# Accumulating w2 as two lines in four column tiles, storing them over two queues, and awaiting the output behind the closing barrier

## The chip, the cores and the metric

The kernel runs on one core of a Trainium2 chip. The metric is the device time of one execution in microseconds (us); a kernel's time is the median of its runs. The times in the profile count from the first instruction of the profiled execution; its span is about 1.3 to 2 us shorter than the measured time.

The names of the parts, as the kernel and the profile have them: PE is the matrix engine, DVE the vector engine, ACT the scalar engine, GpSimd (POOL) a further engine that has little to do here (6.0 us busy in the kernel before). SP issues transfers (DMAs) and waits for them; the profile counts them on 16 DMA engines. PE's sums stand in the tiles named ps, which the kernel puts into PSUM; it puts the other operands into SBUF. A drain is an engine's wait for its own work to end (DVE's of the kernel before starts at 419.7 us and lasts 0.32 us, over its last operation, 419.73 to 420.01); the closing barrier is the point at the end of the kernel's block that each engine passes only when all have come to it. The granted clock is the share of PE's full clock that it was given (0.50 or 1.00 in each record).

## The reference

One decode step of a transformer block, batch 2, one query position: a modulated layer norm, grouped attention over a cache of 32768 keys and values, and a two-layer MLP. Cut to what matters here:

```python
mod = (_silu(c) @ w_mod).reshape(c.shape[0], 6, 1, -1)      # sa, ca, ga, sb, cb, gb
...
x = x + ga * _A_ref(h, A_k_cache, A_v_cache, A_wq, A_wo)
h = _layernorm(x, axis=-1) * (1 + cb) + sb
x = x + gb * _B_ref(h, B_w1, B_b1, B_w2, B_b2)              # w1: 1024 x 3584, w2: 3584 x 1024
return x                                                    # (2, 1, 1024) bf16, 4 KB
```

## The kernel before

All weights and the cache come in pieces of up to 2 MB through one DMA queue, issued by SP, into a ring of 160 KB per partition. A loop over the eight (batch, group) pairs does the attention; behind it stand, fully unrolled, wo, two layer norms, w1, the gelu and w2. The change touches the last of these. The pieces of w2 (the last full one holds slices 16 to 23, the two small ones 24 to 26 and 27):

```python
    w2_v = B_w2.rearrange("(q p j) n -> p q (j n)", p=128, j=4)
    for k, off in enumerate((80, 112, 128)):
        add(("w2", k), [2, 4 * DM], w2_v[:, 2 * k:2 * k + 2, :], off * KB)
    add(("w2", 3), [3 * DM], w2_v[:, 6, 0:3 * DM], 144 * KB)
    add(("w2", 4), [DM], w2_v[:, 6, 3 * DM:4 * DM], 150 * KB)
```

w2 itself: the first 16 slices of 128 rows are multiplied with N = 512 into four column tiles of one PSUM bank, copied to SBUF and turned into columns; the last 12 slices are multiplied as columns, with the weights as the stationary operand, 96 matmuls of 2 columns:

```python
    for q in range(4):
        it = need("w2", q // 2)
        for j in range(4):
            for hf in range(2):
                t = 2 * (j % 2) + hf
                pe(lambda e, w=it.view, q=q, j=j, hf=hf, t=t: e.matmul(psS[0][32 * t:32 * t + 32, :], lhsT=gT[:, 4 * q + j, :],
                                                                       rhs=w[:, q % 2, j * DM + hf * 512:j * DM + (hf + 1) * 512],
                                                                       start=(q == 0 and j < 2), stop=(q == 3 and j >= 2), skip_group_check=True),
                   reads=[it.reg, "gT"], writes=["psS0"], mark=(j == 3 and hf == 1))
    load_row("dve", psS[0], "psS0", 3)
    to_columns(psO, "psO", 3, True, False)
    for q in range(4, 7):
        for j in range(4):
            it = need("w2", 2 if q < 6 else 3 if j < 3 else 4)
            w = it.view.rearrange("p a n -> p (a n)") if q < 6 else it.view
            for k in range(KT8):
                lo = ((q - 4) * 4 + j if q < 6 else j if j < 3 else 0) * DM + k * 128
                pe(lambda e, w=w, q=q, j=j, k=k, lo=lo: e.matmul(psO[:, 2 * k:2 * k + 2], lhsT=w[:, lo:lo + 128], rhs=gT[:, 4 * q + j, 0:2],
                                                                 start=False, stop=(q == 6 and j == 3), skip_group_check=True),
                   reads=[it.reg, "gT"], writes=["psO"], mark=(q > 4 and j in (2, 3) and k == KT8 - 1))
```

Then the gate, the residual, a turn into 16 rows, and the store, which SP awaits inside the block, ahead of the block's closing barrier:

```python
    dve(lambda e: e.tensor_tensor(mT[:, :, :], psO[:, 0:16].rearrange("p (k b) -> p k b", b=2), mod(5), ALU.mult), reads=["psO", "modT"], writes=["mT"])
    dve(lambda e: e.tensor_tensor(res_bf.rearrange("p b k -> p k b"), mT[:, :, :], x1b[:, :, :], ALU.add), reads=["mT", "x1b"], writes=["res_bf"])
    pe(lambda e: e.matmul(psM[0:16, 0:128], lhsT=res_bf.rearrange("p b k -> p (b k)"), rhs=ident[:, :], start=True, stop=True),
       reads=["res_bf", "ident"], writes=["psM"])
    dve(lambda e: e.tensor_copy(res16[:, :], psM[0:16, 0:128]), reads=["psM"], writes=["res16", "c16"])

    s_out = nc.alloc_semaphore("s_out")
    T.wait("sp", reads=["res16"])
    T.raw("sp", lambda e: e.dma_start(out.rearrange("b o (k p) -> (b o k) p", p=128), res16[:, :]).then_inc(s_out, 16))
    T.raw("sp", lambda e: e.wait_ge(s_out, 16))

    with nc.Block() as block:
        T.emit(block)
```

`x1b` (the residual plus the gated bias) is computed ahead of this on DVE; the biases are turned by PE at k == 1 of the w1 stage.

## Time and profile before

| | before |
|---|---|
| median | 423.7 us (423.6 to 423.91) |
| span of the profiled execution | 421.8 us |
| share of the queue that loads, of 16 engines' span | 99.1% |
| last full w2 piece landed | 415.98 us |
| last w2 matmul ended | 418.90 us |
| store issued, landed, span ended | 420.04, 421.44, 421.83 us |

From the page of the kernel before: two of the queues (packets, MB, share of 16 engines' span), and the shares of the chain of work that ended last.

```profile
q1 hardware_dynamic: 14322, 178.29, 99.1%
q8 instruction: 9, 0.15, 0.1%
...
DMA 80%; PE 16%; ACT 2%; SPq 1%; issue 0%; DVE 0%
```

The stream of loads (q1) is the bound.

The chain that ended last, in order of time (start us, us, what), its end:

```profile
385.85 30.13 DMA w<-in_B_w_dram
...
416.02 2.88 PE psO L757 x96
...
419.73 0.28 DVE c L764
```

DMA up to 415.98 us, then 96 matmuls, then (left out up to the last) three DVE operations and one matmul in a row, then the store. The issues of the last loads and of the store (KB each, us from issue to landing):

```profile
w<-in_B_w_dram SPq DMA_DIRECT2D x3, 2048.0 KB, 30.6
w<-in_B_w_dram SPq DMA_DIRECT2D x1, 768.0 KB, 28.0
w<-in_B_w_dram SPq DMA_DIRECT2D x1, 256.0 KB, 23.8
...
out_dram<-c SPq DMA_DIRECT2D x1, 4.0 KB, 1.4
```

And what the instruction queue moved from 416 to 418.6 us (packets, MB, share of 16 engines over the stretch):

```profile
q8 instruction: 1, 0.02, 2.4%
```

One packet falls in this stretch, behind the landing at 415.98; from 412 to 416 us there is none, and the load queue has 98.8% to itself. The packet's share, 2.4% of 16 engines over 2.6 us, is 1.0 us of one engine's time (0.024 x 16 x 2.6).

### The profile page before, as it was taken

Reading aid. Unit: us, or ns where it says so; the run is one execution under the profiler, and the core shown is the slowest. Engines: PE = TensorE matmul, PEld = TensorE weight load, DVE = VectorE, ACT = ScalarE, POOL = GpSimd, SP = SyncE. Lnnn points to the kernel's source line nnn. Section 1 sums busy time; section 2 is a strip of 40 time slices with the busy share of each in tenths; the row PEclk is TensorE's granted clock in tenths of the full one; section 3 lists DMA queues with packets and bytes.
Section 4 is the critical chain, followed back from the end, with each engine's and each line's share of the span. In section 5 each row is a group of like instructions: output and inputs, shape, how many; then the busy total and the mean of one; then the engine's idle time right before and its main releaser. Section 6 shows DMA issues by size and latency. Waiting matters only on the chain.

```text
span 421.8 us, 11638 instructions
## 1 busy us (share of the span) xinstructions
PE 299.5 (71%) x5171; PEld 238.1 (56%) x5171; DVE 167.1 (40%) x347; ACT 156.6 (37%) x269; POOL 6.0 (1%) x31
## 2 busy tenths in 40 slices
PE   1547478878997688587877848796888682445576
PEld 1105158866975678476767828684776671112244
DVE  1102026644663476155534724652474352101311
ACT  2000025547645349142833633383447245000020
POOL 3000000000000000000000000000000000000000
PEclk9999999969989999796988997898899696655565
DMA  8999999999999999999999999999999999999995
GB/s 334 429 431 423 435 432 423 429 432 426 433 432 429 435 429 430 435 429 429 435 429 432 437 423 433 435 426 433 433 428 433 430 430 435 427 429 424 428 423 244
DMA packets 14335, 178.47 MB, mean 423 GB/s; under 512 B 1513, under 2 KB 1520, under 8 KB 2802
## 3 DMA queue, kind: packets, MB, share of 16 engines
q1 hardware_dynamic: 14322, 178.29, 99.1%
q8 instruction: 9, 0.15, 0.1%
q14 instruction: 4, 0.03, 0.0%
HBM read 178.28 MB, written 0.00 MB: 423 GB/s over the span
## 4 chain that ended last, share of the span: by engine, by line
DMA 80%; PE 16%; ACT 2%; SPq 1%; issue 0%; DVE 0%
DMA K<-in_A_k_cache_dram 60%; PE psKT L542 11%; DMA wo<-in_A_wo_dram 8%; DMA w<-in_B_w_dram 7%; DMA wmod<-in_w_mod_dram 4%; PE psS L554 3%; ACT E_sb L575 1%; PE psO L584 1%; SPq L415 1%; ACT KT_sb L546 1%; PE psO L757 1%; PE psS L678 0%; ACT L575 0%; PE psM L565 0%; ACT S_sb L558 0%
## 5 line engine op out<-in xcount | busy, mean ns | idle before, releaser
L542 PE MATMUL psKT<-ident,K 128*128 128x128 bf16 x2048 | 173.8, 237 | 39.0 <-DMA K<-in_A_k_cache_dram 37.8
L542 PEld LDWEIGHTS psKT<-ident,K 128*128 128x128 bf16 x2048 | 133.2, 106 | 49.7 <-DMA K<-in_A_k_cache_dram 44.9
L548 DVE COPY KT_sb<-psKT 128x1024 bf16<-128x1024 bf16 x160 | 108.3, 689 | 112.5 <-PE psKT L542 112.5
L546 ACT ACTIVATE KT_sb<-psKT 128x1024 bf16<-128x1024 bf16 x96 | 98.0, 1020 | 131.2 <-PE psKT L542 131.2
L554 PE MATMUL psS<-qcur,KT_sb 128*128 128x8 bf16 x2048 | 88.2, 167 | 8.1 <-ACT KT_sb L546 6.7
L554 PEld LDWEIGHTS psS<-qcur,KT_sb 128*128 128x128 bf16 x2048 | 79.5, 99 | 13.2 <-ACT KT_sb L546 8.1
L584 PE MATMUL psO<-V,E_sb 128*32 128x512 bf16 x512 | 35.5, 403 | 6.3 <-DMA V<-in_A_v_cache_dram 5.0
L575 ACT ACTIVATE E_sb<-S_sb,negm 128x256 bf16<-128x256 f32 x64 | 32.3, 504 | 7.7 <-DVE negm L571 6.8
L559 DVE TENSOR_REDUCE m1c<-psS 128x8 f32<-128x512 f32 x32 | 22.1, 691 | 14.4 <-ACT S_sb L558 13.3
L558 ACT ACTIVATE S_sb<-psS 128x512 f32<-128x512 f32 x32 | 19.0, 592 | 14.1 <-PE psS L554 14.1
L584 PEld LDWEIGHTS psO<-V,E_sb 128*32 128x32 bf16 x512 | 11.5, 100 | 16.8 <-DMA V<-in_A_v_cache_dram 5.7
L491 PE MATMUL psS<-wmod,inT 128*32 128x512 bf16 x64 | 8.4, 622 | 11.9 <-DMA wmod<-in_w_mod_dram 11.9
L678 PE MATMUL psS<-wo,atT 128*32 128x512 bf16 x64 | 7.6, 627 | 11.3 <-DMA wo<-in_A_wo_dram 11.3
L462 ACT ACTIVATE stat<-stat 128x2 f32<-128x2 f32 x3 | 0.6, 204 | 38.9 <-DVE stat L461 38.9
L512 PE MATMUL psS<-wq,inT 128*32 128x512 bf16 x64 | 7.6, 627 | 6.9 <-DMA wq<-in_A_wq_dram 5.9
L575 ACT ACTIVATION_READ_ACCUMULATOR E_sb<-S_sb,negm 128x1 f32 x64 | 12.1, 189 | 0.0
L491 PEld LDWEIGHTS psS<-wmod,inT 128*32 128x32 bf16 x64 | 1.3, 112 | 17.9 <-DMA wmod<-in_w_mod_dram 17.4
L678 PEld LDWEIGHTS psS<-wo,atT 128*32 128x32 bf16 x64 | 1.9, 128 | 16.3 <-DMA wo<-in_A_wo_dram 10.3
L604 PE MATMUL psM<-msum,hmat 128*128 128x128 f32 x16 | 4.4, 359 | 7.1 <-DVE msum L599 7.1
L497 ACT ACTIVATE S_sb<-psS 128x512 f32<-128x512 f32 x1 | 0.6, 597 | 22.8 <-DVE S_sb L499 22.8
L499 DVE COPY S_sb<-psS 128x512 f32<-128x512 f32 x1 | 0.7, 692 | 20.6 <-PE psS L491 20.6
L599 DVE SCALAR_TENSOR_TENSOR msum<-psO,mk,msum 128x128 f32<-128x128 f32 x24 | 8.4, 351 | 0.8
(116 smaller groups left out, 132.3 us busy)
## 6 DMA issues: line engine op xcount, KB each, us to landing
K<-in_A_k_cache_dram SPq DMA_DIRECT2D x32, 2048.0 KB, 31.6
V<-in_A_v_cache_dram SPq DMA_DIRECT2D x32, 2048.0 KB, 35.1
wmod<-in_w_mod_dram SPq DMA_DIRECT2D x8, 1536.0 KB, 16.5
wq<-in_A_wq_dram SPq DMA_DIRECT2D x4, 2048.0 KB, 37.5
wo<-in_A_wo_dram SPq DMA_DIRECT2D x4, 2048.0 KB, 29.0
w<-in_B_w_dram SPq DMA_DIRECT2D x4, 1792.0 KB, 39.1
w<-in_B_w_dram SPq DMA_DIRECT2D x3, 2048.0 KB, 30.6
w<-in_B_w_dram SPq DMA_DIRECT2D x1, 768.0 KB, 28.0
```

What stands on the lines that cost most here:

```text
L491: pe(lambda e, w=it.view, k=k, ch=ch, n=n, q=q: e.matmul(bank[n][32 * q:32 * q + 32, :], lhsT=inT[:, k, :], rhs=w[:, ch * 512:(ch + 1) * 512],
L512: pe(lambda e, w=it.view, k=k, ch=ch, n=n, q=q: e.matmul(bank[n][32 * q:32 * q + 32, :], lhsT=inT[:, k, :], rhs=w[:, k % 2, ch * 512:(ch + ...
L542: pe(lambda e, kq=kq, jj=jj, w=it.view, t=t: e.transpose(psKT[kq][:, jj * 128:(jj + 1) * 128], w[:, t, :], ident[:, :]), reads=[it.reg, "i ...
L546: act(lambda e, src=src: e.activation(KT_sb[g8][:, :, :], src, ACT.Copy), reads=[f"psKT{kq}"], writes=[f"KT_sb{g8}"], sem=f"ev{cc}_{g8}")
L548: dve(lambda e, src=src: e.tensor_copy(KT_sb[g8][:, :, :], src), reads=[f"psKT{kq}"], writes=[f"KT_sb{g8}"], sem=f"ev{cc}_{g8}")
L554: pe(lambda e, t=t, jj=jj: e.matmul(ps[:, t * HPG:(t + 1) * HPG], lhsT=KT_sb[g8][:, jj, :], rhs=qcur[:, :], start=True, stop=True), reads= ...
L558: act(lambda e: e.activation(Sc, ps[:, :].rearrange("p (t h) -> p h t", h=HPG), ACT.Copy), reads=[preg], writes=[f"S_sb{i % 2}_{cc}"], sem ...
L559: dve(lambda e: e.tensor_reduce(m1c[:, :, cc], ps[:, :].rearrange("p (t h) -> p h t", h=HPG), AX.X, ALU.max), reads=[preg], writes=[f"m1c{ ...
L575: act(lambda e: e.activation(E_sb[:, :, h, :], S_sb[j][:, h, :].rearrange("p (u t) -> p u t", t=4), ACT.Exp, bias=negm[:, h:h + 1], scale= ...
L584: pe(lambda e, t4=t4, tg=tg, q=q: e.matmul(psO[32 * q:32 * q + 32, :], lhsT=E_sb[:, tg // 4, :, :].rearrange("p h t -> p (h t)"), rhs=it.v ...
L599: dve(lambda e, q=q: e.scalar_tensor_tensor(out=msum[:, :], in0=psO[:, q * 128:(q + 1) * 128], scalar=mk4[:, q:q + 1], in1=msum[:, :], op0 ...
L678: pe(lambda e, w=it.view, g=g, j=j, hf=hf, q=q: e.matmul(psS[0][32 * q:32 * q + 32, :], lhsT=atT[g][:, j, :], rhs=w[:, j, hf * 512:(hf + 1 ...
```

## The change

Its intent is to shorten what follows the last landing. All 28 slices of w2 go through the four-column-tile form, with 256 columns per tile, so that the two batches' results stand as lines on partitions 32q and 32q+1 and need no turn into columns and back; the gate and the residual are turned into the same lines in the shade of earlier waits; each batch's four lines are stored straight from there, one batch from SP's queue and one from ACT's; SP awaits the stores behind the closing barrier. Cut to its core:

```diff
+    def to_lines(src, reg, base, k0, k1):
+        for k in range(k0, k1):
+            q = k // 2
+            pe(lambda e, k=k, q=q: e.matmul(psM[32 * q:32 * q + 32, 256 + (k % 2) * 128:384 + (k % 2) * 128],
+                                            lhsT=src[:, base + k:base + k + 16, :].rearrange("p k b -> p (k b)"), rhs=identf[:, :], start=True, stop=True),
+               reads=[reg, "identf"], writes=["psM"], mark=(k == k1 - 1))
+
+    def keep_lines(n, name):
+        dve(lambda e: e.tensor_copy(flat[:, n * 256:(n + 1) * 256], psM[:, 256:512]), reads=["psM"], writes=[name] + FLAT)
@@ behind the matmuls of wo's group g
+        if g == 0:
+            biases()                       # moved here from the w1 stage
+        else:
+            to_lines(modT, "modT", 5 * KT8, 3 * (g - 1), min(3 * g, 8))
+    keep_lines(0, "gate")
@@ in the w1 stage
-        if k == 1:
-            ... the turn of the biases
+        if k in (3, 5):
+            to_lines(x1b, "x1b", 0, k - 3, k - 1)
@@ w2
-    ... both halves of w2, load_row, to_columns, mT, res_bf, the turn into 16 rows
+    for f in range(FT):
+        ... it, w, lo: the piece and the place of slice f
+        for t in range(4):
+            pe(lambda e, w=w, f=f, t=t, lo=lo: e.matmul(psS[0][32 * t:32 * t + 32, 0:256], lhsT=gT[:, f, :], rhs=w[:, lo + t * 256:lo + (t + 1) * 256],
+                                                        start=(f == 0), stop=(f == FT - 1), skip_group_check=True),
+               reads=[it.reg, "gT"], writes=["psS0"], mark=(f % 8 == 7 or f > FT - 3) and t == 3)
+        if f in (7, 15):
+            to_lines(x1b, "x1b", 0, f // 8 * 2 + 4, f // 8 * 2 + 6)
+    keep_lines(1, "base")
+    res = qrow[0:98, 0:256]
+    dve(... flat[0:98, 512:768] = psS[0][0:98, 0:256] * gate lines)
+    dve(... res = that + base lines)
@@ the store
-    T.wait("sp", reads=["res16"])
-    T.raw("sp", lambda e: e.dma_start(out.rearrange("b o (k p) -> (b o k) p", p=128), res16[:, :]).then_inc(s_out, 16))
-    T.raw("sp", lambda e: e.wait_ge(s_out, 16))
-
-    with nc.Block() as block:
+    for b, E in enumerate(("sp", "act")):
+        T.wait(E, reads=["res"])
+        T.raw(E, lambda e, b=b: e.dma_start(out[b].rearrange("o (q n) -> (o q) n", q=4), qrow[b:98:32, 0:256]).then_inc(s_out, 16))
+
+    with nc.Block(no_gpsimd_drain=True) as block:
         T.emit(block)
+    nc.sync.wait_ge(s_out, 32)
```

More of the change, by code (lines that the diff above doesn't have):

```diff
@@ L287, in bass_adaLN_cond__gqa_block_cached__mixer_channel_mlp__decode_kernel @@
     x16 = sb("x16", [16, 128], BF16)
-    c16 = sb("c16", [16, 128], BF16)
+    x1b = sb("x1b", [128, KT8 + 16, 2])
+    xT = sb("xT", [128, KT8, 2])
     rsum16 = sb("rsum16", [128, HPG, 16])
@@ L297, in bass_adaLN_cond__gqa_block_cached__mixer_channel_mlp__decode_kernel @@
     b2m = sb("b2m", [KT8, 128], BF16)
-    xT = sb("xT", [128, KT8, 2])
     b1T = sb("b1T", [128, FT])
@@ L308, in bass_adaLN_cond__gqa_block_cached__mixer_channel_mlp__decode_kernel @@
     t1 = sb("t1", [128, KT8, 2])
-    modT = sb("modT", [128, NMOD, 2])
+    modT = sb("modT", [128, NMOD + 16, 2])
     qT = sb("qT", [128, 2, HQ], BF16)
@@ L315, in bass_adaLN_cond__gqa_block_cached__mixer_channel_mlp__decode_kernel @@
     x1T = sb("x1T", [128, KT8, 2])
-    x1b = sb("x1b", [128, KT8, 2])
     hmid = sb("hmid", [128, KT8, 2])
@@ L321, in bass_adaLN_cond__gqa_block_cached__mixer_channel_mlp__decode_kernel @@
     gT = sb("gT", [128, FT, 32], BF16)
-    mT = sb("mT", [128, KT8, 2])
-    res_bf = sb("res_bf", [128, 2, KT8], BF16)
-    res16 = c16
     m1c = sb("m1c", [128, HPG, NCH])
@@ L334, in bass_adaLN_cond__gqa_block_cached__mixer_channel_mlp__decode_kernel @@
     ROW = [f"S_sb0_{cc}" for cc in range(NCH)]
+    flat = S_sb[1].rearrange("p h n -> p (h n)")
+    FLAT = [f"S_sb1_{cc}" for cc in range(NCH)]
     E_sb = sb("E_sb", [128, NT // 4, HPG, 4], BF16)
@@ L437, in bass_adaLN_cond__gqa_block_cached__mixer_channel_mlp__decode_kernel @@
     T.inst("pool", lambda e: e.memset(onesf[:, :], 1.0), writes=["onesf"])
-    for t, nm in [(inT, "inT"), (gT, "gT")] + [(atT[g], f"atT{g}") for g in range(G)]:
+    for t, nm in [(inT, "inT"), (gT, "gT"), (modT, "modT"), (x1b, "x1b")] + [(atT[g], f"atT{g}") for g in range(G)]:
         T.inst("pool", lambda e, t=t: e.memset(t[:, :, :], 0.0), writes=[nm])
@@ L505, in bass_adaLN_cond__gqa_block_cached__mixer_channel_mlp__decode_kernel @@
                reads=[f"mrow{n}", "identf"] + ROW, writes=["psM"], mark=(i == 3))
-    dve(lambda e: e.tensor_copy(modT[:, :, :], psM[:, 0:2 * NMOD].rearrange("p (j b) -> p j b", b=2)), reads=["psM"], writes=["modT"])
+    dve(lambda e: e.tensor_copy(modT[:, 0:NMOD, :], psM[:, 0:2 * NMOD].rearrange("p (j b) -> p j b", b=2)), reads=["psM"], writes=["modT"])
     modulate(inT[:, :, 0:2], "inT", 0, 1)
@@ L669, in bass_adaLN_cond__gqa_block_cached__mixer_channel_mlp__decode_kernel, with biases @@
     extract()
+    def biases():
+        for j in range(4):
+            pe(lambda e, j=j: e.matmul(psM[:, 16 + 7 * j:23 + 7 * j], lhsT=b1m[:, j::4], rhs=ident[0:7, 0:7], start=True, stop=True),
+               reads=["b1m", "ident"], writes=["psM"], mark=False)
+        pe(lambda e: e.matmul(psM[:, 44:52], lhsT=b2m[:, :], rhs=ident[0:KT8, 0:KT8], start=True, stop=True),
+           reads=["b2m0", "b2m1", "b2m3", "b2m7", "ident"], writes=["psM"])
+        dve(lambda e: e.tensor_copy(b1T.rearrange("p (q j) -> p j q", j=4), psM[:, 16:44].rearrange("p (j q) -> p j q", j=4)), reads=["psM"], writes=["b1T"])
+        dve(lambda e: e.tensor_copy(b2T[:, :], psM[:, 44:52]), reads=["psM"], writes=["b2T"])
+    def to_lines(src, reg, base, k0, k1):
[6 more added lines that the diff above has]
+        dve(lambda e: e.tensor_copy(flat[:, n * 256:(n + 1) * 256], psM[:, 256:512]), reads=["psM"], writes=[name] + FLAT)
     for g in range(G):
@@ L704, in bass_adaLN_cond__gqa_block_cached__mixer_channel_mlp__decode_kernel @@
     dve(lambda e: e.tensor_copy(inT[:, :, 0:2], xc[:, :, :]), reads=["xc"], writes=["inT"])
+    xb = x1b[:, 0:KT8, :]
+    dve(lambda e: e.tensor_tensor(xb, mod(5), b2T[:, :].unsqueeze(2).to_broadcast([128, KT8, 2]), ALU.mult), reads=["modT", "b2T"], writes=["x1b"])
+    dve(lambda e: e.tensor_tensor(xb, xb, x1T[:, :, :], ALU.add), reads=["x1b", "x1T"], writes=["x1b"])
     zbank, zreg = [psS[1], psO], ["psS1", "psO"]
@@ L713, in bass_adaLN_cond__gqa_block_cached__mixer_channel_mlp__decode_kernel @@
                reads=[it.reg, "inT"], writes=[zreg[n]], mark=(ch in (3, 6)))
-        if k == 1:
-            for j in range(4):
-                pe(lambda e, j=j: e.matmul(psM[:, 16 + 7 * j:23 + 7 * j], lhsT=b1m[:, j::4], rhs=ident[0:7, 0:7], start=True, stop=True),
-                   reads=["b1m", "ident"], writes=["psM"], mark=False)
-            pe(lambda e: e.matmul(psM[:, 44:52], lhsT=b2m[:, :], rhs=ident[0:KT8, 0:KT8], start=True, stop=True),
-               reads=["b2m0", "b2m1", "b2m3", "b2m7", "ident"], writes=["psM"])
-            dve(lambda e: e.tensor_copy(b1T.rearrange("p (q j) -> p j q", j=4), psM[:, 16:44].rearrange("p (j q) -> p j q", j=4)), reads=["psM"], writes=["b1T"])
-            dve(lambda e: e.tensor_copy(b2T[:, :], psM[:, 44:52]), reads=["psM"], writes=["b2T"])
+        if k in (3, 5):
+            to_lines(x1b, "x1b", 0, k - 3, k - 1)
     load_row("act", psS[1], "psS1", 1)
@@ L729, in bass_adaLN_cond__gqa_block_cached__mixer_channel_mlp__decode_kernel @@
                reads=[f"row{n + 1}", "identf"] + ROW, writes=["psM"], mark=(j == 3))
-    dve(lambda e: e.tensor_tensor(x1b[:, :, :], mod(5), b2T[:, :].unsqueeze(2).to_broadcast([128, KT8, 2]), ALU.mult), reads=["modT", "b2T"], writes=["x1b"])
-    dve(lambda e: e.tensor_tensor(x1b[:, :, :], x1b[:, :, :], x1T[:, :, :], ALU.add), reads=["x1b", "x1T"], writes=["x1b"])
     dve(lambda e: e.tensor_tensor(zT[:, :, :], psM[:, 0:2 * FT].rearrange("p (f b) -> p f b", b=2), b1T[:, :].unsqueeze(2).to_broadcast([128, FT, 2]), ALU.add),
@@ L738, in bass_adaLN_cond__gqa_block_cached__mixer_channel_mlp__decode_kernel @@
     dve(lambda e: e.tensor_tensor(gT[:, :, 0:2], sg[:, :, :], zT[:, :, :], ALU.mult), reads=["sg", "zT"], writes=["gT"])
-    for q in range(4):
-        it = need("w2", q // 2)
-        for j in range(4):
-            for hf in range(2):
-                t = 2 * (j % 2) + hf
-                pe(lambda e, w=it.view, q=q, j=j, hf=hf, t=t: e.matmul(psS[0][32 * t:32 * t + 32, :], lhsT=gT[:, 4 * q + j, :],
-                                                                       rhs=w[:, q % 2, j * DM + hf * 512:j * DM + (hf + 1) * 512],
-                                                                       start=(q == 0 and j < 2), stop=(q == 3 and j >= 2), skip_group_check=True),
-                   reads=[it.reg, "gT"], writes=["psS0"], mark=(j == 3 and hf == 1))
@@ L749, in bass_adaLN_cond__gqa_block_cached__mixer_channel_mlp__decode_kernel @@
-    load_row("dve", psS[0], "psS0", 3)
-    to_columns(psO, "psO", 3, True, False)
-    for q in range(4, 7):
-        for j in range(4):
-            it = need("w2", 2 if q < 6 else 3 if j < 3 else 4)
-            w = it.view.rearrange("p a n -> p (a n)") if q < 6 else it.view
-            for k in range(KT8):
-                lo = ((q - 4) * 4 + j if q < 6 else j if j < 3 else 0) * DM + k * 128
-                pe(lambda e, w=w, q=q, j=j, k=k, lo=lo: e.matmul(psO[:, 2 * k:2 * k + 2], lhsT=w[:, lo:lo + 128], rhs=gT[:, 4 * q + j, 0:2],
-                                                                 start=False, stop=(q == 6 and j == 3), skip_group_check=True),
-                   reads=[it.reg, "gT"], writes=["psO"], mark=(q > 4 and j in (2, 3) and k == KT8 - 1))
@@ L760, in bass_adaLN_cond__gqa_block_cached__mixer_channel_mlp__decode_kernel @@
-    dve(lambda e: e.tensor_tensor(mT[:, :, :], psO[:, 0:16].rearrange("p (k b) -> p k b", b=2), mod(5), ALU.mult), reads=["psO", "modT"], writes=["mT"])
-    dve(lambda e: e.tensor_tensor(res_bf.rearrange("p b k -> p k b"), mT[:, :, :], x1b[:, :, :], ALU.add), reads=["mT", "x1b"], writes=["res_bf"])
-    pe(lambda e: e.matmul(psM[0:16, 0:128], lhsT=res_bf.rearrange("p b k -> p (b k)"), rhs=ident[:, :], start=True, stop=True),
-       reads=["res_bf", "ident"], writes=["psM"])
-    dve(lambda e: e.tensor_copy(res16[:, :], psM[0:16, 0:128]), reads=["psM"], writes=["res16", "c16"])
+    for f in range(FT):
+        q, j = f // 4, f % 4
+        it = need("w2", q // 2 if q < 6 else 3 if j < 3 else 4)
+        w, lo = (it.view.rearrange("p a n -> p (a n)"), (f % 8) * DM) if q < 6 else (it.view, (j if j < 3 else 0) * DM)
+        for t in range(4):
[4 more added lines that the diff above has]
+            to_lines(x1b, "x1b", 0, f // 8 * 2 + 4, f // 8 * 2 + 6)
@@ L766, in bass_adaLN_cond__gqa_block_cached__mixer_channel_mlp__decode_kernel @@
+    keep_lines(1, "base")
+    res = qrow[0:98, 0:256]
+    dve(lambda e: e.tensor_tensor(flat[0:98, 512:768], psS[0][0:98, 0:256], flat[0:98, 0:256], ALU.mult), reads=["psS0", "gate"] + FLAT, writes=["gated"])
+    dve(lambda e: e.tensor_tensor(res, flat[0:98, 512:768], flat[0:98, 256:512], ALU.add), reads=["gated", "base"] + FLAT, writes=["res", "E_sb"])
     s_out = nc.alloc_semaphore("s_out")
-    T.wait("sp", reads=["res16"])
-    T.raw("sp", lambda e: e.dma_start(out.rearrange("b o (k p) -> (b o k) p", p=128), res16[:, :]).then_inc(s_out, 16))
```

## The prediction

> **What bounds the kernel.** The DMA stream. The page gives 178.47 MB at 423 GB/s over a 421.8 us span, and the queue takes 99.1% of 16 engines' span; the chain of work that ended last is 80% DMA. The change touches only the tail. In narrow windows DMA keeps about 425 GB/s until 416.4 us, then about 200 GB/s until 418.0, then nothing. The last full w2 piece lands at 415.98, and the piece with j 0 to 2 (issued 389.9, 28.0 us to landing) at about 417.95: the 96 small w2 matmuls (416.02 to 418.91, about 28 ns each) show a pause of some 0.2 us just there. After it come 32 matmuls (0.9 us), then the chain DVE 0.19, DVE 0.24, PE 0.29, DVE 0.28 (store issued at 420.04), 1.4 us to landing, and 0.36 us from landing to the end of the span (421.8): SP's drain and the closing barrier.
>
> **What the change does.**
> 1. w2: all 28 slices become four 256-column matmuls in four column tiles. Present four-tile rounds of 512 columns last 0.427 us at the half clock, so a slice should take 0.213 us, 0.107 at full clock. [...] After the landing at 417.95 four slices are left: by estimate 3 x 0.213 + 0.40 = 1.03 us cold, 0.6 us warm, against 0.94 now. So it gains 0 to 0.35 us, not 2: most of the 96 matmuls hide under the DMA already.
> 2. Gone: the mid-way copy and turn into columns (413.1 to 415.7), in DMA shade, worth nothing; mT, res_bf, PE transpose, cast (1.11 us to the store). New: two 98x256 fp32 DVE operations, estimate 0.45 us each from 0.17 us at 16 and 0.22 at 56 columns: gain about 0.05.
> 3. Output: the barrier passes under the store's 1.4 us; gain about 0.3 us.
> 4. Added in front: gate lines. Two float32 turns behind the last wo matmul (from the pair at L565/L604: about 0.21 us a pass cold, so 0.85 us and drain) and a 0.43 us copy stand on DVE ahead of the row copy: +1.3 us on the layernorm chain. In w1 +1.7 us of turns at the half clock less 0.25 of biases, partly given back by the full clock. w2 then begins at about 410.5 to 412 instead of 409.34. Its first 24 slices and two turns need at most 6.8 us (cold): slack before 417.95 takes nearly all of it.
>
> **Sum.** 0.15 + 0.05 + 0.3 = 0.5 us: 423.2 us, range 422.4 to 423.9. Over 2% faster 0.01, within 2% 0.98, slower 0.01.
>
> **What would show each step.** (1) the last w2 landing unchanged near 418.0; PE waits for DMA before the last four slices, which then take 0.6 to 1.05 us. (2) last matmul to store issue about 1.0 us. (3) the span ends within 0.15 us of the landing. (4) the row copy after wo starts about 1.3 us later (387.5), w2 at 410.5 to 412, without moving the end.
>
> **What would make it wrong.** w2 starting after 412 with the half clock kept: then PE, not DMA, ends last, and the change costs up to 1 us. A store from ACT's unused queue landing later than 1.4 us. The DMA stream's end moving by itself. A full clock at w2's end: then 422.8.

What the trace shows is that in the kernel before the granted clock was 0.50 from 364.12 to 401.66 us and 1.00 from there to 405.08, the w1 stage having begun at 396.44. 0.15 + 0.05 + 0.3 = 0.5 us less than the 423.7 before, so 423.2. "Cold" is the half clock, "warm" the full one. The estimates of 1.03 and 0.6 us use a last slice of 0.40 us whose source the record doesn't give; the trace agrees, as a round of 512 columns ended 0.62 us after its start at the half clock, 0.21 of it for the columns that a slice doesn't have. A "pass" is one of the two matmul records that a float32 turn has in the trace (32 for the 16 turns of L681 in the changed kernel, 0.21 us from one to the next at the half clock).

## More of the kernel before

A DMA tells of its landing through a semaphore, a counter, which rises 16 times for each piece in the traces.

## The result

The changed kernel takes 424.82 us (424.67 to 425.11, 6 runs) against 423.73 us (6 runs) before: ratio 1.0026, 95% interval 1.0013 to 1.0039. That is 1.1 us slower, outside the predicted 422.4 to 423.9, though within 2%. (A ratio is the mean time of one kernel's fast runs over that of the other's of the same rounds, so it isn't quite the ratio of the medians quoted.)

The page after, the same parts:

```profile
q1 hardware_dynamic: 14298, 178.28, 98.9%
q8 instruction: 9, 0.15, 0.1%
...
DMA 80%; PE 16%; ACT 2%; SPq 1%; issue 0%; DVE 0%
```

The load queue's bytes and the number of instruction packets are as before, and so is the chain in shares. The end of the chain, in order of time:

```profile
385.81 31.44 DMA w<-in_B_w_dram
...
417.30 2.91 PE psS L762 x28
...
420.69 0.42 DVE E_sb L770
```

The stretch that ends with the last full w2 piece now lasts to 417.25 instead of 415.98, and the matmuls behind it last as long as before (2.91 against 2.88 us). PE's wait for the piece, from the timeline:

```profile
417.30 2.88 PE L762 MATMUL psS<-w,gT 128*32 128x256 bf16 x48 [3.62 <-DMA w<-in_B_w_dram]
```

The landings of w2:

```profile
w<-in_B_w_dram SPq DMA_DIRECT2D x3, 2048.0 KB, 31.4
w<-in_B_w_dram SPq DMA_DIRECT2D x1, 768.0 KB, 29.2
w<-in_B_w_dram SPq DMA_DIRECT2D x1, 256.0 KB, 25.0
```

The two small pieces take 1.2 us longer each. The full pieces' 31.4 against 30.6 is a median of three and hides which of them it is. None of these last three pieces was issued more than 0.06 us later, and no byte was added. The trace holds the times at which each piece's semaphore rose, once for each of 16 parts. For the last full w2 piece, the last three of the 16 (us), beside the start of the third late packet of the instruction queue:

```
kernel          13 parts by   14th    15th    16th     instruction packet
before          415.72        415.83  415.95  415.98   417.81
changed         415.80        415.87  416.04  417.25   414.81
```

Fifteen parts are where they were, and one is 1.2 us late. The two small pieces have one late part each as well (they end at 419.09 and 419.70 us instead of 417.83 and 418.46), and PE waits for both again; so its end, too, stands behind the very last landing. In the stretch from 412 to 416 us the queues moved:

```profile
q1 hardware_dynamic: 244, 1.65, 98.4%
q8 instruction: 1, 0.02, 1.5%
```

The packet of the instruction queue now lies in the stretch ahead of the landing, and none follows from 416 to 418.6 us, where before it lay behind it (1.5% of 16 engines over 4 us is 0.96 us of one engine). That is a coincidence until it is moved on purpose.

The tail behind PE changed as well. The two DVE operations took 0.42 us each, so the store was issued 0.93 us behind the last matmul instead of 1.14. The issue of the stores in the changed kernel, then in the kernel before (start, us, engine, line):

```profile
421.14 0.62 SPq L775 DMA_DIRECT2D out_dram<-E_sb  x1
421.14 1.36 ACTq L775 DMA_DIRECT2D out_dram<-E_sb  x1
```

```profile
420.04 0.35 SPq L768 DMA_DIRECT2D out_dram<-c  x1
```

The last store landed at 423.08, 1.94 us after its issue, against 1.40 before; and the span ended 0.04 us behind it instead of 0.39. Summed up: 1.31 - 0.21 + 0.54 - 0.35 = 1.29 us, the difference of the spans (423.12 - 421.83).

### The profile page after: what moved, and what is told of

Its sections match the earlier page's. It is cut to its first block, busy times and chain, and to the rows that moved or that the text cites. A ratio compares the mean times of both kernels' runs of the same rounds, so it can differ in the third digit from the quotient of the medians.

```text
span 423.1 us, 11661 instructions
## 1 busy us (share of the span) xinstructions
PE 299.0 (71%) x5178; PEld 241.5 (57%) x5178; DVE 167.7 (40%) x347; ACT 157.1 (37%) x269; POOL 6.2 (1%) x33
## 4 chain that ended last, share of the span: by engine, by line
DMA 80%; PE 16%; ACT 2%; SPq 1%; issue 0%; DVE 0%
DMA K<-in_A_k_cache_dram 60%; PE psKT L540 11%; DMA wo<-in_A_wo_dram 8%; DMA w<-in_B_w_dram 7%; DMA wmod<-in_w_mod_dram 4%; PE psS L552 3%; ACT E_sb L573 1%; PE psO L582 1%; SPq L413 1%; ACT KT_sb L544 1%; PE psS L762 1%; ACT L573 0%; PE psS L695 0%; PE psM L563 0%; ACT S_sb L556 0%
## 5 line engine op out<-in xcount | busy, mean ns | idle before, releaser
L540 PE MATMUL psKT<-ident,K 128*128 128x128 bf16 x2048 | 176.0, 238 | 39.7 <-DMA K<-in_A_k_cache_dram 38.1
L540 PEld LDWEIGHTS psKT<-ident,K 128*128 128x128 bf16 x2048 | 134.7, 107 | 50.3 <-DMA K<-in_A_k_cache_dram 45.2
L552 PEld LDWEIGHTS psS<-qcur,KT_sb 128*128 128x128 bf16 x2048 | 80.5, 99 | 12.4 <-ACT KT_sb L544 7.9
L582 PE MATMUL psO<-V,E_sb 128*32 128x512 bf16 x512 | 34.6, 395 | 4.1 <-DMA V<-in_A_v_cache_dram 2.8
L695 PE MATMUL psS<-wo,atT 128*32 128x512 bf16 x64 | 6.7, 566 | 9.6 <-DMA wo<-in_A_wo_dram 9.6
L762 PE MATMUL psS<-w,gT 128*32 128x256 bf16 x112 | 6.9, 417 | 5.0 <-DMA w<-in_B_w_dram 3.6
## 6 DMA issues: line engine op xcount, KB each, us to landing
w<-in_B_w_dram SPq DMA_DIRECT2D x3, 2048.0 KB, 31.4
```

What stands on the lines that cost most here:

```text
L540: pe(lambda e, kq=kq, jj=jj, w=it.view, t=t: e.transpose(psKT[kq][:, jj * 128:(jj + 1) * 128], w[:, t, :], ident[:, :]), reads=[it.reg, "i ...
L552: pe(lambda e, t=t, jj=jj: e.matmul(ps[:, t * HPG:(t + 1) * HPG], lhsT=KT_sb[g8][:, jj, :], rhs=qcur[:, :], start=True, stop=True), reads= ...
L582: pe(lambda e, t4=t4, tg=tg, q=q: e.matmul(psO[32 * q:32 * q + 32, :], lhsT=E_sb[:, tg // 4, :, :].rearrange("p h t -> p (h t)"), rhs=it.v ...
L695: pe(lambda e, w=it.view, g=g, j=j, hf=hf, q=q: e.matmul(psS[0][32 * q:32 * q + 32, :], lhsT=atT[g][:, j, :], rhs=w[:, j, hf * 512:(hf + 1 ...
L762: pe(lambda e, w=w, f=f, t=t, lo=lo: e.matmul(psS[0][32 * t:32 * t + 32, 0:256], lhsT=gT[:, f, :], rhs=w[:, lo + t * 256:lo + (t + 1) * 25 ...
```

## The experiments

The theory (called "fetch" in the expectations): PE's own program is fetched in packets of 16 KB through one of the DMA engines that carry the weights; a packet ahead of the last w2 pieces makes one of their 16 parts late, and the change moved PE's instructions so that the third packet behind the loop came too early. That was inferred, from the name that the profile gives the queue and from the one late part. What the traces show: each of these packets is 16384 bytes, the three behind the loop take 0.93, 0.93 and 0.96 us in the changed kernel and 0.94, 0.92 and 1.01 before, and from one to the next PE started 303 and 247 instructions in the changed kernel, 274 and 291 in the kernel before. The expectations of a_n144 and a_m72 rested on a fixed count of instructions between packets as well; no trace shows one. Rival 1: PE has more work and is late. Rival 2: the piece is late for a reason that has nothing to do with PE's program.

Rival 1 was dead from the trace already: PE waited 3.6 us for the piece (the line of 417.30 us above). Rival 2 needed experiments.

### Three tests that were none: a_n144, a_n48, b_n96

```diff
+        for _ in range(24 if k in (1, 2, 3, 4, 5, 6) else 0):    # 8 in a_n48, 16 in b_n96
+            T.raw("pe", lambda e: e.nop())
```

a_n144:

> The changed kernel with 144 PE no-ops put into the DMA waits of the w_mod stage, so that every later PE instruction stands 144 places further in PE's program. Theory (fetch): in the changed kernel a 16 KB packet of the instruction queue runs for 0.96 us at 414.81 us, and one of the 16 parts of the last three w2 pieces lands 1.2 us after the other 15. [...] the shift moves this one behind the w2 landings (to about 417 or later). Then the last full w2 piece lands near 416.05, PE ends near 419.0 and the time falls by about 1.2 us to 423.6. Rival 1 (PE work: gate and base lines and the column tiles make PE late) and rival 2 (the piece is late for a reason that has nothing to do with PE's program): no-ops change nothing, 424.8, the piece lands at 417.25 again.

a_n48:

> The changed kernel with only 48 no-ops in the same place. Theory (fetch): the packet comes earlier, at about 411 us, still ahead of the last full w2 piece, with another one less than 30 us before it as now; one part of that piece stays late by about 1.2 us and the time stays at 424.8 (within 0.3). Rivals 1 and 2: 424.8 as well. If no-ops as such helped, it would be faster as with 144.

b_n96:

> The kernel before, with 96 no-ops in the w_mod stage. Theory (fetch): its last packet, at 417.81 us, comes 96 PE instructions earlier, at about 413 to 415.5 us, ahead of the last full w2 piece; that piece lands at about 417.2 instead of 415.98, the 96 small matmuls start then, and the time rises by about 1.2 us to 424.9. Rivals: unchanged, 423.7.

Measured: 424.73, 424.88 and 423.58 us, each as the kernel that it was made from (the kernel before in the same rounds: 423.67), and the third late instruction packet stayed within 0.4 us of where it was. I took this at first as a sign that only instructions behind the loop count, and the next expectation says so. That was wrong. The built program holds no no-op: PE's list has 1161 entries in the changed kernel, in a_n144 and in a_n48, and 1164 in the kernel before and in b_n96. The no-ops were dropped on the way. The three runs are repeats of the two kernels and say only that the delay is there each time: one part of the last full w2 piece landed at 417.21 and 417.33 us in the first two, and all parts by 416.01 in the third. Whether instructions ahead of the loop would move the packets was not tried.

### Moving the packet with real instructions: a_m72, a_m24, b_m48

```diff
                    reads=[it.reg, f"atT{g}"], writes=["psS0"], mark=(j == 7 and hf == 1))
+        for _ in range(24 if g in (0, 1, 2) else 0):             # 8 in a_m24, 16 in b_m48
+            pe(lambda e: e.matmul(psS[1][0:32, 0:8], lhsT=ident[:, 0:32], rhs=ident[:, 0:8], start=True, stop=True),
+               reads=["ident"], writes=["psS1"], mark=False)
```

Each small matmul is two PE instructions (weight load and matmul; the page of the kernel before counts 5171 of each), stands in a wait for wo, and its result is overwritten.

> The kernel before with 48 such matmuls (96 PE instructions), 16 behind each of three wo groups. Theory (fetch): the packet of 417.8 us comes at 411 to 415 us, the last full w2 piece lands near 417.2 instead of 415.98, PE starts the last 96 matmuls then, and the time rises by about 1.2 us to 424.9. Rivals: 423.7.

Measured: 424.83 us (before 423.65), ratio 1.0028 (1.0012 to 1.0045). The kernel before became as slow as the changed one by 96 idle instructions. Its chain, and the instruction queue from 412 to 416 us:

```profile
385.86 31.31 DMA w<-in_B_w_dram
...
417.22 2.85 PE psO L760 x96
```

```profile
q8 instruction: 1, 0.02, 1.5%
```

The packet came at 414.73, one part of the piece at 417.18 with the other 15 by 415.88, and the 96 matmuls, as long as ever, started 1.2 us later. Nothing of w2 or of the store was changed here, so rival 2 falls.

> The changed kernel with 24 such matmuls (48 PE instructions), 8 behind each of three wo groups. Theory (fetch): the packet comes one or two us earlier (410 to 413.5), still ahead of the last full w2 piece and about 15 to 20 us after the one before it: one part late, landing near 417.2, time 424.8 as the changed kernel. Rivals: the same. If the small matmuls helped in themselves[...] it would be faster like the one with 72.

Measured: 424.83 us, as expected: packets at 387.92 and 413.18, the last part at 417.46. The small matmuls do not help in themselves.

> No-ops ahead of the main loop moved no packet of the instruction queue: the three late ones (363 to 364, 399 to 400, 415 or 418 us) stand at the same count of PE instructions behind the loop[...]. So the shift has to be made behind the loop. Here: the changed kernel with 72 small matmuls of the identity (144 PE instructions with their weight loads), 24 behind each of the first three wo groups, where PE waits for DMA; their result is thrown away. Theory (fetch): the packet of 414.8 us comes at the third quarter of w2, about 417.5 us or later, behind the w2 landings; the one of 399 us at about 402 to 405, one more in the wo stage. The last full w2 piece lands near 416.05, PE ends near 419.0, time 423.6 (1.2 us less than the changed kernel). Rivals (PE work, or lateness that has nothing to do with PE's program): landing at 417.25, time 424.8 or more.

Measured: 424.79 us, not 423.6. The expectation was wrong, the theory not: I had assumed that packets go on at a fixed count of instructions, so that 144 more would bring a fourth into w2's end and push the third far back. There are three packets behind the loop in all, of nine in the run (that PE's program then ends is presumed, not shown); 144 more instructions moved the second from 398.88 to 382.88 and the third from 414.81 to 408.78. A packet there is still ahead of the piece. Here even the piece before that one had one part late (412.45, the other 15 by 410.97), as the theory has it: the delay lasts from piece to piece. In the changed kernel, too, the last part of the three pieces behind the packet rose 1.21, 1.20 and 1.18 us after the 15th. In all three runs the added instructions moved the third packet to an earlier time (from 417.81 to 414.73 in b_m48, from 414.81 to 413.18 in a_m24 and 408.78 in a_m72); so the next runs have fewer.

### Fewer instructions: a_drop14 and a_drop14_m57

```diff
-        for t in range(4):
+        for t in range(4) if not 0 < f < 15 else ():             # wrong result on purpose
```

a_drop14_m57 has the same edit and 19 small matmuls behind each of three wo groups.

> The changed kernel without the matmuls of w2's slices 1 to 14 (wrong result on purpose): 112 PE instructions fewer behind the loop and ahead of the wait for the last full w2 piece; all DMAs as before. PE was idle for 3.6 us ahead of that wait, so the missing work itself can save nothing. Theory (fetch): the third late packet of the instruction queue[...] moves from 414.8 us to 417.5 or later or doesn't come; the last full w2 piece lands near 416.05 (all 16 parts together), PE ends near 419.0, time 423.6 or a little less, 1.2 below the changed kernel. Rival (the piece is late for a reason that has nothing to do with PE's program, such as where the buffers lie or how the stores or the queues are set up): landing at 417.25 again, time 424.8.

> The same, with 57 small matmuls (114 PE instructions) put into the wo stage's waits, so that the count of PE instructions is that of the changed kernel again. Theory (fetch): the packet comes ahead of the last full w2 piece again (408 to 415 us), one part of it lands at about 417.25, time 424.8. Rival (a_drop14 was faster because work was left out): as fast as a_drop14.

Measured: 423.5 us and 424.77 us, in the same rounds, before 423.58. (Both were reported as correct: presumably w2's term is so small in these data that the comparison doesn't see 14 missing slices, so it doesn't vouch for w2 in the other runs either.) The chains, first a_drop14, then a_drop14_m57:

```profile
385.81 30.07 DMA w<-in_B_w_dram
...
415.93 2.97 PE psS L762 x37
```

```profile
385.64 31.66 DMA w<-in_B_w_dram
...
417.35 2.90 PE psS L765 x38
```

The first has eight instruction packets in the whole run instead of nine, none behind 398.87 us, and all 16 parts landed by 415.88. The twin does the same w2 work with the instruction count restored: packet at 409.99, one part at 417.30. So the 1.27 us between them belong to the count of PE's instructions and not to the work left out.

### A right kernel with fewer instructions: a_pad and a_pad2

In two places, for the gate and for the residual, eight turns of 32 columns become two of 128 (48 PE instructions fewer: the 16 turns of L681 stand in the changed kernel's trace as 32 weight loads and 32 matmuls, so each of the 12 saved is four); in a_pad2 the rows of wo and w1 are turned in bf16 as well (72 fewer: the 12 turns of L713 and L746 have 24 matmul records there in float32, where the 112 bf16 matmuls of L762 have 112).

```diff
+    pad = [flat[:, 1024 + 256 * i:1280 + 256 * i].rearrange("p (h q r) -> p h q r", h=2, q=4) for i in range(2)]   # zeroed
+        dve(... pad[i][:, :, :, 0:2] = src, for the gate and for x1b)
-    def to_lines(src, reg, base, k0, k1):
-        for k in range(k0, k1): ...                              # 8 matmuls
+    def to_lines(i):
+        for h in range(2):
+            pe(lambda e, h=h: e.matmul(psM[:, 256 + h * 128:384 + h * 128], lhsT=pad[i][:, h, :, :].rearrange("p q r -> p (q r)"), rhs=identf[:, :], start=True, stop=True), ...)
```

> A repair of the changed kernel with a right result: the gate and base lines are turned by 2 matmuls of 128 columns each (from a tile with zeros between the columns) instead of 8 of 32 columns, so 48 PE instructions fewer behind the loop, all of them ahead of the wait for the last full w2 piece; the gate copy stands earlier. Theory (fetch): the third late packet stands some 48 instructions later, a few slices behind that wait, or is not needed. The last full w2 piece lands whole near 416.05. If the packet comes at about 416.5 to 417.5 us, one part of the last two small pieces is still late by up to 1.2 us and the time is 424.0 to 424.5; if it doesn't come, 423.4 to 423.6. Rival (only leaving work out helped in a_drop14): 424.8.

> The same, and the rows of the wo and w1 results are kept in bf16 for their turn into columns, one pass each instead of two: 72 PE instructions fewer in all. Theory (fetch): the third packet comes at 417.5 us or later or not at all; every w2 part lands as in the kernel before (416.05, 417.85, 418.5); PE ends near 418.9; time 423.3 to 423.6, 1.2 to 1.5 us below the changed kernel. It should still not reach the 422.7 of the kernel before with the wait moved: two stores of four rows, 0.62 us of issue each and one after the other, hold the last landing and the barrier. Rival: 424.8.

Measured: 423.62 and 423.59 us (before 423.65): 1.2 us below the changed kernel, and equal to the kernel before. The third packet came at 417.91 and 417.74 us, later than I had thought for a_pad, and no part was late (415.98, 417.83, 418.47 us for the three last pieces of a_pad). The end of a_pad's chain:

```profile
389.90 27.93 DMA w<-in_B_w_dram
...
417.87 1.07 PE psS L770 x16
```

This is the step (1) that I had predicted: PE has done slices 16 to 23, waits for the small piece at 417.83, and needs 1.07 us for the last four slices. It ends at 418.94, against 418.90 in the kernel before. So the new form of w2 gains nothing behind the landing. The prediction left out one thing here: the very last slice comes in a piece of its own, which landed at 418.47 us (418.46 before). Its matmuls started at 418.51 in a_pad and at 418.54 in the kernel before, so a faster rate ahead of it had almost nothing left to gain. The repair is equal to before although its wait is moved behind the barrier; where that gain went is the next question.

### The wait: b_wait, bw_drain, b_nodrain

b_wait is the kernel before with the wait alone moved (and, as in the change, without the drain of GpSimd that the block's end has by default):

```diff
-    T.raw("sp", lambda e: e.wait_ge(s_out, 16))
-    with nc.Block() as block:
+    with nc.Block(no_gpsimd_drain=True) as block:
         T.emit(block)
+    nc.sync.wait_ge(s_out, 16)
```

> The kernel before with only the wait for the output moved behind the closing barrier (and no drain of GpSimd), the store itself as it was. My step 3: from the landing of the store to the end of the span are 0.36 us now; behind the barrier 0.02 to 0.05 should be left. Time 423.4 (0.3 less). Rival: what ends the measured time lies outside the span and takes as long either way, 423.7.

Measured: 422.71 us (422.67 to 422.78; before 423.65), ratio 0.9978 (0.9961 to 0.9994). It gains 0.94 us where 0.3 was expected, and is faster than both kernels. But b_wait changes two things. bw_drain has the wait moved and the drain kept (`nc.Block()`), b_nodrain has the drain dropped and the wait where it was:

```diff
     # bw_drain, against b_wait
-    with nc.Block(no_gpsimd_drain=True) as block:
+    with nc.Block() as block:
     # b_nodrain, against the kernel before
-    with nc.Block() as block:
+    with nc.Block(no_gpsimd_drain=True) as block:
```

> b_wait moved the wait behind the barrier and also left out GpSimd's drain at the end of the block, so its 0.94 us belong to two edits. This is b_wait with that drain back. Theory A (the place of the wait is what counts: GpSimd's drain lies at 373 us, long before the end): 422.7 us. Theory B (the drain costs at the end): up to 423.65.

> The kernel before without GpSimd's drain, its wait inside the block as it was. Theory A: 423.65 us, as the kernel before. Theory B: the part of the 0.94 us that bw_drain loses, so down to 422.7.

Measured, in the same rounds, with the kernel before at 423.70: bw_drain 422.74 us, ratio 0.9977 (0.9960 to 0.9993); b_nodrain 423.83 us, ratio 1.0003 (0.9987 to 1.0020). The gain belongs to the place of the wait, and the drain is worth nothing.

The closing barrier as DVE passes it, first before, then in b_wait, then in the changed kernel (engine, instruction, count, ns each, then the first and the last start in us; the last is the passing of the barrier):

```profile
L771 DVEq EVENT_SEMAPHORE  x1: 21/21/21, 421.8 to 421.8; - x1
```

```profile
L770 DVEq EVENT_SEMAPHORE  x2: 21/21/21, 420.0 to 420.7; - x2
```

```profile
L777 DVEq EVENT_SEMAPHORE  x2: 21/21/21, 421.2 to 422.9; - x2
```

In b_wait DVE is through at 420.7, 1.1 us earlier than before; SP alone stays until the landing, to 421.4. In the changed kernel, with its wait behind the barrier too, DVE is through at 422.9 only.

### The stores: a_sp2, bw_act, bw_2q, bw_s4, bw_s4adj

a_sp2 is the changed kernel with both stores issued by SP (`("sp", "sp")` in the loop over the batches):

> The changed kernel with both halves of the output stored from SP's queue, none from ACT's. In the changed kernel the stores are issued at 421.14 us and the last lands at 423.08, 1.94 us later, against 1.40 us for the one store before; ACT's issue took 1.36 us, SP's 0.62. Theory (ACT's queue is slow on its first use): both from SP in turn, 0.35 to 0.62 us of issue each, the last landing 1.6 to 2.0 us after the first issue, time 424.5 to 424.9, so faster by 0 to 0.3. Rival (the shape, four rows of 512 bytes, is slow, whatever the queue): two of them in turn on one queue, landing 2.2 us or more after issue, time 425.1 or more.

Measured: 424.89 us, against 424.82 for the changed kernel. That is the upper end of what the theory allowed and too fast for its rival, so the run alone decides nothing. The issue of both from SP (x2, their busy time together):

```profile
421.40 1.16 SPq L775 DMA_DIRECT2D out_dram<-E_sb  x2
```

One such store costs SP 0.5 to 0.6 us, against 0.35 for the one store of 16 rows. Taking ACT's queue away doesn't help. bw_act is b_wait with its one store of 16 rows issued by ACT:

> The same kernel with its one store of 16 rows issued from ACT instead of SP. Theory (ACT's first issue is slow): issue 1.0 to 1.4 us, last landing 0.5 us or more later than from SP, time 423.3 to 423.7. Rival (fewer than 16 rows in one DMA is what is slow, on either queue): 0.35 us of issue and 422.7 to 422.8.

Measured: 422.68 us, as b_wait. The issue took ACT 0.38 us, and the store landed 1.44 us after its start. My theory that ACT's first issue is slow falls. bw_2q is b_wait with the 16 rows halved:

```diff
-    T.raw("sp", lambda e: e.dma_start(out.rearrange("b o (k p) -> (b o k) p", p=128), res16[:, :]).then_inc(s_out, 16))
+    for b, E in enumerate(("sp", "act")):
+        ... the 8 rows of batch b from engine E
```

> The kernel before with the wait behind the barrier (422.7 us in its run), its store now in two halves of 8 rows, one from SP's queue and one from ACT's. Theory (ACT's first issue is slow, 1.36 us in the changed kernel, and its drain holds the closing barrier): ACT's issue takes 1.2 to 1.4 us, the barrier ends about 1 us later, the last landing is 0.4 to 0.6 us later, time 423.4 to 423.7. Rival (it is the shape of four rows alone): issue of both about 0.35 to 0.4 us, time 422.7.

Measured: 422.85 us (before 423.58), 0.14 above b_wait. The two stores of 8 rows:

```profile
419.96 0.31 SPq L769 DMA_DIRECT2D out_dram<-c  x1
419.96 0.64 ACTq L769 DMA_DIRECT2D out_dram<-c  x1
```

ACT's takes twice SP's, as the 1.36 of the changed kernel is about twice its 0.62: factors of 2.1 and 2.2 for two stores issued at the same moment, as if ACT's were done after SP's; two in a row from SP took 1.16 us together. That the one waits for the other is my reading; no run shows the wait itself. What was left was the shape, 4 rows of 512 bytes on partitions 32 apart. The last two runs give b_wait just that, and then the same rows on neighbouring partitions. Both store other data than the result:

```diff
-    T.raw("sp", lambda e: e.dma_start(out.rearrange("b o (k p) -> (b o k) p", p=128), res16[:, :]).then_inc(s_out, 16))
+    for b, E in enumerate(("sp", "act")):
+        T.raw(E, lambda e, b=b: e.dma_start(out[b].rearrange("o (q n) -> (o q) n", q=4), qrow[b:98:32, 0:256]).then_inc(s_out, 16))
+        # bw_s4adj: qrow[4 * b:4 * b + 4, 0:256]
```

> b_wait (422.71 us) with the two stores of the changed kernel: four rows of 512 bytes, 32 partitions apart, one batch from SP, one from ACT, at the same time as b_wait's store (wrong result on purpose: the rows hold old data). Theory (the form of the stores is what takes the gain of the wait away again): issue 0.62 and 1.36 us, last landing 1.9 us after issue, the barrier about 1 us later, time 423.5 to 423.7. Rival (the two 98-partition DVE operations or something else in the changed form does): 422.7 to 422.9.

> The same with the four rows on neighbouring partitions (wrong result on purpose). If the distance of 32 partitions makes the issue slow: 0.31 and 0.64 us as with 8 rows, time 422.8 to 422.9. If it is the number or the length of the rows: 0.62 and 1.36 us, time as bw_s4.

Measured: 423.81 us for bw_s4, 1.1 above b_wait, and 423.03 us for bw_s4adj, 0.32 above it (both 0.1 us above what was expected). The issues, first bw_s4, then bw_s4adj:

```profile
420.25 0.62 SPq L769 DMA_DIRECT2D out_dram<-E_sb  x1
420.25 1.36 ACTq L769 DMA_DIRECT2D out_dram<-E_sb  x1
```

```profile
420.19 0.29 SPq L769 DMA_DIRECT2D out_dram<-E_sb  x1
420.19 0.62 ACTq L769 DMA_DIRECT2D out_dram<-E_sb  x1
```

In this pair the distance of 32 partitions doubled the issue: 0.62 and 1.36 us against 0.29 and 0.62, and 0.78 of the 1.1 us are due to it. Neighbouring rows of 512 bytes cost what 8 rows of 256 bytes do (0.31 and 0.64). Why the distance matters is not settled. The changed form of the stores takes back, alone, all that the moved wait gave.

How an issue of 1.36 us can cost so much, when the wait is for the landing, shows when the profiled executions are put side by side. The second column is the end of the last store's issue, or, in the first two rows, the landing, which SP awaits inside the block; the third is the passing of the barrier by DVE, the last two the time of the same execution and what remains of it behind the barrier (us):

| kernel | issue ended (landed) | barrier passed | span | time | time less barrier |
|---|---|---|---|---|---|
| before | (421.44) | 421.78 | 421.83 | 423.71 | 1.93 |
| b_nodrain | (421.38) | 421.81 | 421.86 | 423.74 | 1.93 |
| changed | 422.51 | 422.93 | 423.12 | 424.77 | 1.84 |
| a_pad | 421.25 | 421.67 | 421.85 | 423.60 | 1.93 |
| bw_s4 | 421.61 | 422.03 | 422.23 | 423.88 | 1.85 |
| bw_s4adj | 420.81 | 421.22 | 421.59 | 423.07 | 1.85 |
| bw_2q | 420.61 | 421.02 | 421.44 | 422.86 | 1.84 |
| b_wait | 420.32 | 420.74 | 421.40 | 422.78 | 2.04 |
| bw_act | 420.40 | 420.82 | 421.49 | 422.90 | 2.08 |

The barrier passes 0.3 to 0.5 us after the last issue has ended (or the awaited landing), and the time is 1.8 to 1.9 us more, although SP's wait goes on behind the barrier. Only where the issue is short, in the last two rows (and in bw_drain, 2.04), is the time longer than that, and there the landing, the span's end, may be what counts. Of the other ten runs' profiled executions eight have 1.84 to 1.88; two, a_m72 and a_drop14, have 2.17 with a long issue. Both were 0.3 us slower than their kernel's median, and what was longer in them lay outside the span. So moving the wait replaced the landing by the end of the issue; in the kernel before that is a replacement of 1.40 us by 0.35, in the changed kernel of 1.40 by 1.36. What runs behind the barrier no trace shows, so that the barrier sets the time is read from the regularity of most of these executions, with two that depart from it; it isn't shown by an experiment of its own.

## Why the prediction was wrong

- **Where it failed: "the last w2 landing unchanged near 418.0".** The sum of the prediction had -0.15 us for the end of w2. It measured +1.31 (end of PE 418.90 to 420.21). The term was not mis-sized, its sign was wrong, because the landings were taken as given by bytes and bandwidth. Shown: they also depend on the count of PE's instructions, which moves the packets of the instruction queue. 96 idle PE instructions slowed the kernel before by 1.2 us (b_m48); 112 fewer took 1.3 us off the changed kernel, and putting the count back returned them (a_drop14 and its twin); a right kernel with 48 fewer lost the delay (a_pad). Among "what would make it wrong" stood "the DMA stream's end moving by itself"; it moved by the change.
- **Why the second packet (398.88 us, 400.12 before) makes no part late:** the landing times in the kept traces answer this. The parts of a piece land over about 2 us (414.07 to 415.98 for the last full w2 piece before), some well ahead of the others. In the changed kernel 7 parts rose more than 1.05 us ahead of the 13th up to the piece that ended at 364.70, 6 from the piece of 369.61, and 5 from that of 401.34: one fewer behind each of the packets of 364.41 and 398.88. Where the second packet was moved forward the step moved with it (packet at 387.63 in b_m48, step at 392.70; 382.88 in a_m72, step at 388.29). So these packets put back a part that was ahead, unseen at the end; the third (414.81) left the 5 as they were and put back one of the others. **Not shown:** which DMA engine a packet takes, and by what rule; the trace doesn't name engines.
- **Step 1, the rate of w2: right.** With the landings in place (a_pad) four slices were left and took 1.07 us at a granted clock of 0.50, predicted 1.03 at the half clock. The full clock came at the wrong time: in the changed kernel PE had it while it waited and lost it before it went on. Columns: window, its length, busy us of the engines, granted clock, DMA share, GB/s.

```profile
core 0: us, PE busy (x) PEld busy (x) DVE busy (x) ACT busy (x) POOL busy (x), PEclk, DMA share, GB/s
413.50:416.50 3.00, 0.17 (x2) 0.00 (x0) 0.42 (x1) 0.00 (x0) 0.00 (x0) 1.00 0.99 408
417.00:420.20 3.20, 2.88 (x48) 1.49 (x48) 0.00 (x0) 0.00 (x0) 0.00 (x0) 0.53 0.18 72
```

PE's last matmul ended at 413.67 us, and by the clock records the clock was 1.00 from 413.21 and 0.50 from 416.62, so it fell 2.95 us after that matmul. It didn't rise at once with the work either: in the kernel before w1 began at 396.44 and the clock rose at 401.66, 5.2 us later. The changes of the clock in the changed kernel (406.38, 413.21, 416.62, 420.03 us) lie 3.41 us apart or twice that, and none falls on a begin of w2's matmuls (408.95, 417.30) or their end (413.67, 420.21). What rule they follow is not shown.
- **Step 2, the tail on DVE: right in kind.** 0.42 us for each operation (predicted 0.45), gain 0.21 (predicted 0.05).
- **Step 3, the output: "gain about 0.3 us", which measured 0.94 for the moved wait and about -1.1 for the form of the stores.** The first was mis-sized (b_wait, bw_drain): I had counted the 0.36 us from the landing to the end of the span, where the time goes, by the table above, with the moment at which the other engines pass the barrier. The second was missing. The prediction spoke of a late landing from ACT's queue as a risk; what cost the time here is the issue of four rows 32 partitions apart (1.36 us in bw_s4), and the barrier passed 0.42 us behind its end. Step (3) of its signs, "the span ends within 0.15 us of the landing", came true (0.04) and was worth nothing: the span is not the time.
- **Step 4, the work in front: no cost, as predicted, but the times were off.** The row copy started at 386.16 and w2 at 408.95, not at 387.5 and 410.5, because PE had the full clock in the last wo stage of this execution (1.00 from 382.49 to 389.31 us, where the kernel before had 0.50; its 16 matmuls there took 1.05 us, against 1.90). PE was ahead by 3.6 us at the landing either way.

The parts, each from a pair of kernels that lead step by step from before to the changed kernel: +1.2 us for the packet (changed kernel against a_pad), -0.94 for the wait (b_wait against before), +1.1 for the stores (bw_s4 against b_wait), -0.2 for what else is left (a_pad against bw_s4: by argument the shorter end on DVE; bw_s4 also issued its store 0.28 us later than b_wait in the profiled executions, 420.25 against 419.97, so some of its 1.1 may be chance). In all +1.2 us; measured +1.1, the steps being of different rounds.

## What to carry to other kernels

In a kernel whose loads fill the DMA engines (99.1% here), look at the instruction queue's packets in the profile (16384 bytes and 0.92 to 1.01 us each behind the loop), and keep them out of the last microseconds ahead of the final landing, by fewer instructions where the tail is unrolled (48 fewer moved the third from 414.81 to 417.91 us in a_pad). Here the third packets that came from 408.78 to 415.21 us, 1 to 7 us ahead of the landing due at about 416, did harm, about 1.2 us each time, and those at 417.7 or later cost nothing of that size. At the very end, ask when the last engine is through the closing barrier: await the output behind it and store in a form that is short to issue (0.35 us for 16 rows, against 1.36 for the later of two stores of rows 32 partitions apart). Here the move of the wait gave 0.94 us, the only gain of the change that mattered, and the kernel before with this alone (422.71 us) beats both kernels.
